# Wider weight loads for the scores, the transposes and the look-ahead rows, and a planner fed with measured durations

## The chip, the core and the metric

The kernel runs on one core of a Trainium2 chip. The metric is the device time of one execution in microseconds; lower is better. TensorE (PE) does the matmuls, VectorE (DVE), ScalarE (ACT) and GpSimd (POOL) the rest, SyncE (SP) issues the weight DMAs. A matmul on PE is a pair: a weight load, which puts the stationary operand (rows x columns) into the array, and the matmul, which streams the moving operand past it. The profile lists the two as PEld and PE.

## The reference

Four layers, applied one after the other on x of 2048 tokens x 640: A, B, A, B, each on a layer norm of x and added to x. B is a mixer MLP; A is attention in 64 segments of 32 tokens, where each segment also reads 8 memory rows that the segment before it produced. So the segments of one A layer can't run side by side.

```python
for s in range(n_seg):                       # 64 segments, in order
    h = concat([mem, x[segment s]])          # 8 + 32 = 40 rows x 640
    q, k, v = h @ Wq, h @ Wk, h @ Wv         # 32 heads of 192
    scores = where(mask, q @ k.T * 192**-0.5, -1e9)
    p = softmax(scores);  o = (p @ v) @ Wo
    mem = o[:8];  out.append(o[8:])
# B: h = gelu(ln(x) @ w1); four column groups of h shifted by -1, +1, -2, +2 tokens
#    x1 = x + shifted @ w2;  x + (x1 - x) + gelu(ln(x1) @ w3) @ w4
```

## The kernel before, in words

**Two lanes.** All four layers run in one pass. Lane 0 is the first A layer, lane 1 the second, five segments behind (`LAG`). Step t does segment t of lane 0 and segment t-5 of lane 1 together, so that each weight is loaded once for both. There are 69 steps: 0 to 4 have lane 0 alone, 5 to 63 have both, 64 to 68 have lane 1 alone. In a two-lane step a moving operand is N = NS = 80 columns wide (2 x 40), in a one-lane step N = 40. Every second step also runs one chunk of the B layers: 64 tokens of each lane, interleaved, so 128 rows.

**An attention step** (`attention_step`, L502) goes over four pairs of groups of four heads. For each group: 30 projection matmuls each for k, q and v (L532, weights 128x128, moving N columns); `pss`, the scores, six matmuls whose stationary operand is qT, N columns wide (L594); the masked minimum and scaling on DVE (L605), exp on ACT (L612), sums, reciprocal and product on DVE (L616 to L618); `pst`, four transposes of the probabilities, which load Pm as N x N weights (L626); the copy PT on ACT (L631); `pvt`, six transposes of v, which load vF N columns wide and stream 128 (L569); `pso`, eight matmuls with V as N x 128 weights (L640); the copy oT on DVE (L646); 30 output matmuls into `psy` (L657). qT, vF, Pm and PT exist once, kT, V twice, oT eight times. At the step's end ACT copies the new memory rows from `psy` to hT (L675), which the next step's first projection needs.

**The B chunk** (`chunk`, L812) transposes yTB (`psx`, L823) and, for the next chunk's first rows, the four columns behind it (`psl`, L830, weights 128 x 4 columns). The look-ahead rows lie in `lnx`: rows 0 to 3 the look-ahead, rows 32 to 95 the next segments of x; `psvl` (L880, through `transposes`, L722) transposes all 96 rows at once. Then w1, w2, w3, w4 (L905, L950, L985, L1011).

**What sets the order.** Nothing is issued as it stands in the source. Each operation is an entry `add(engine, duration, due, function, reads, writes)` of a `Plan` (L76). `place()` (L124) simulates all engines with these hand-written durations, with `LAT` between engines, `PE_LAT` behind PE, a DMA rate and the PSUM slots (six of class A, two of class B), and always takes the entry that can start first, by due time among those within 0.12 us on PE or 0.05 us elsewhere. The result is one fixed order for each engine. For a weight DMA that the plan starts at its own pace it adds a wait on the last PE operation that the plan has finished by then (L1105 to L1112), and a streamed DMA goes into a ring of eight slots. So a changed duration moves instructions on all five engines and the PE operations that release the weight DMAs. 31 streamed loads of 384 KB belong to each attention step; the other parts of the attention weights stay resident.

These lines carry the parts that the change touches:

```python
def mm_us(n, m=128, k=1):                     # L408, the plan's price of k matmuls
    return k * (max(54, n) / 2400.0 + 0.0025)
lhsT=q[:, c, 0:N], rhs=k_[:, j:j + w_, 0:N]   # L595, pss
transpose(out=o[0:N, i, 0:N], in_=Pb[0:N, i, 0:N], identity=ident[0:N, 0:N])   # L626, pst
lhsT=V_[0:N, ...], rhs=Pt[0:N, 2 * hf + i2, 0:N]                               # L640, pso
```

Of the kernel before, what the change touches and what calls it, by code (L numbers as in the profile page):

```python
# [30 lines left out]
LAT = 0.1  # L31
PE_LAT = 0.23
# [208 lines left out]
def kernel(  # L241
# [97 lines left out]
    nc.vector.memset(lnA[0:32, 0:1], 1.0 + EPS)  # L339
    nc.vector.memset(lnA[0:32, 1:2], EPS * EPS)  # L340

    hT = [ctile([P, KC, NS], bf16, f"hT{i}") for i in range(4)]
    qT = ctile([P, GC, NS], bf16, "qT")
    vF = ctile([P, GC, NS], bf16, "vF")
    kT = [ctile([P, 8, NS], bf16, f"kT{i}") for i in range(2)]
    Vt = [ctile([NS, 2 * VP], bf16, f"V{i}") for i in range(2)]
    Pm = ctile([NS, HG, NS], bf16, "Pm")
# [15 lines left out]
    lnx = h2u[0:96, Dm:2 * Dm]  # L363
# [9 lines left out]
    nc.gpsimd.memset(yTB[:], 0.0)  # L373
    nc.gpsimd.memset(xres[:], 0.0)
# [41 lines left out]


# [84 lines left out]
    def attention_step(t):  # L502
# [13 lines left out]
        def proj_pair(pr):  # L516
            s0 = base + sl * 2 * pr
            for kind, off in (("k", 0.0), ("q", 0.2), ("v", 0.5)):
                wbs, wv = load_pair(kind, pr, s0 + off * 2 * sl, LEAD_A)
                for j in range(2):  # L520
# [17 lines left out]
                    if kind == "q":  # L538
                        q = qT

                        def fq(op, pq=pq, q=q):
                            nc.scalar.copy(out=q[:, :, 0:N], in_=T(pq)[:, :, 0:N])  # L542
                        add("ACT", act_us(GC * N), due, fq, r=(pq,), w=(B("qT"),))
                    elif kind == "k":
                        k_ = kT[G % 2]

                        def fk(op, pq=pq, k_=k_):
                            p4 = T(pq)[:].rearrange("p (h c) n -> p h c n", h=2)
                            k4 = k_[:].rearrange("p (h c) n -> p h c n", h=2)
                            nc.vector.tensor_copy(out=k4[:, :, 0::3, 0:N], in_=p4[:, :, 0::2, 0:N])  # L550
                        add("DVE", dve_us(4 * N), due, fk, r=(pq,), w=(B("kT", G % 2, 0),))
                        for part, (r0, r1, jj) in enumerate(((0, 64, 1), (64, P, 2))):
                            def fk2(op, pq=pq, k_=k_, r0=r0, r1=r1, jj=jj):
                                p4 = T(pq)[:].rearrange("p (h c) n -> p h c n", h=2)
                                k4 = k_[:].rearrange("p (h c) n -> p h c n", h=2)
                                nc.vector.tensor_copy(out=k4[r0:r1, :, jj, 0:N], in_=p4[r0:r1, :, 1, 0:N])  # L556
                            add("DVE", dve_us(2 * N), due, fk2, r=(pq,), w=(B("kT", G % 2, 1 + part),))
                    else:
                        vf, V_ = vF, Vt[G % 2]

                        def fvf(op, pq=pq, vf=vf):
                            nc.scalar.copy(out=vf[:, :, 0:N], in_=T(pq)[:, :, 0:N])  # L562
                        add("ACT", act_us(GC * N), due, fvf, r=(pq,), w=(B("vF"),))
                        pvt = ps("A", [NS, GW], bf16, "pvt")

                        def fvt(op, pvt=pvt, vf=vf):
                            o = T(pvt)
                            for c in range(GC):
                                nc.tensor.transpose(out=o[0:N, c * P:(c + 1) * P], in_=vf[:, c, 0:N], identity=ident[:, :])  # L569
                        add("PE", mm_us(P, k=GC), due + 0.1 * sl, fvt, r=(B("vF"),), w=(pvt,))  # L570
                        for hf in range(2):
                            def fe(op, pvt=pvt, V_=V_, hf=hf):
                                src = T(pvt)[0:N, GWH * hf:GWH * (hf + 1)].rearrange("n (a b) -> n a b", a=2)
                                v0 = hf * (VP - 64)
                                dst = V_[0:N, v0:v0 + 512].rearrange("n (a b) -> n a b", a=2)[:, :, 64 * hf:64 * hf + Dh]
                                if hf:
                                    nc.vector.tensor_copy(out=dst, in_=src)
                                else:
                                    nc.scalar.copy(out=dst, in_=src)  # L579
                            add("DVE" if hf else "ACT", dve_us(GWH) if hf else act_us(GWH), due, fe, r=(pvt,),  # L580
                                w=(B("V", G % 2, hf),))

        def attend(g):
# [3 lines left out]
            pss = ps("A", [NS, HG * NS], f32, "pss")  # L587
            hi = s0 + 0.5 * sl

            def fs(op):  # L590
                o = T(pss)
                seq = [(0, 1, 0, 0), (1, 1, 2, 3), (2, 1, 3, 4), (3, 1, 5, 7), (0, 2, 1, 1), (2, 2, 4, 5)]
                for n_, (i, w_, c, j) in enumerate(seq):
                    nc.tensor.matmul(out=o[0:N, i * N:(i + w_) * N].rearrange("p (a b) -> p a b", a=w_),  # L594
                                     lhsT=q[:, c, 0:N], rhs=k_[:, j:j + w_, 0:N],  # L595
                                     start=(n_ == 0), stop=(n_ == len(seq) - 1), skip_group_check=True)
# [11 lines left out]
            add("DVE", dve_us(HG * N) + 0.1, hi - 4, f1, r=(pss,), w=(pss, smk))  # L608
# [4 lines left out]
            add("ACT", act_us(HG * N), hi - 4, f2, r=(pss, smk), w=(Pk,))  # L613
# [6 lines left out]
            add("DVE", 0.42 + 0.17 + 0.45, hi - 4, f3, w=(Pk, B("sm4", G % 2)))  # L620
            pst = ps("A", [NS, HG, NS], bf16, "pst")

            def f4(op):
                o = T(pst)
                for i in range(HG):
                    nc.tensor.transpose(out=o[0:N, i, 0:N], in_=Pb[0:N, i, 0:N], identity=ident[0:N, 0:N])  # L626
            add("PE", mm_us(N, N, 4), hi - 3, f4, r=(Pk,), w=(pst,))
            Pt = PT

            def f5(op):  # L630
                nc.scalar.copy(out=Pt[0:N, :, 0:N], in_=T(pst)[0:N, :, 0:N])  # L631
# [3 lines left out]
            def f6(op):  # L635
                o = T(pso)
                for hf in range(2):
                    for i2, col, c, st, sp in ((0, 0, 0, True, True), (0, 128, 1, True, False), (1, 192, 1, False, True),
                                               (1, 320, 2, True, True)):
                        nc.tensor.matmul(out=o[:, 3 * hf + c, 0:N], lhsT=V_[0:N, VP * hf + col:VP * hf + col + P],  # L640
                                         rhs=Pt[0:N, 2 * hf + i2, 0:N], start=st, stop=sp)
# [45 lines left out]
    def ln_ops(src, rows, st, stk, srck, due, const_cols):  # L687
# [16 lines left out]
        add("DVE", 2 * 0.47 + 0.19 + 0.28, due, f1, r=(srck,), w=(stk,))  # L704
# [5 lines left out]
        add("POOL", 0.7, due, f2, w=(stk,))  # L710

    def apply_ln(dst, src, rows, st, col, dstk, srck, stk, due, us=0.6):
# [12 lines left out]
    def gelu(pz, n, due, outs, w, a=(), own=None):  # L725
# [28 lines left out]
        add("DVE", dve_us(n * XB) + 0.15 * (len(outs) - 1), due, f4, r=(pz, gk), w=w)  # L754
# [8 lines left out]
    def chunk_loads(c, part):  # L763
# [23 lines left out]
        if edge:  # L787
            def fz(op):
                nc.gpsimd.memset(xres[:] if part == "x" else lnx[0:4, :], 0.0)
# [7 lines left out]
        for lane, k0 in look if part == "l" else ():  # L797
            def f(op, lane=lane, k0=k0):
                nc.gpsimd.dma_start(out=lnx[lane:4:2, :], in_=src[lane][k0:k0 + 2, :])
# [3 lines left out]
        if s < NSEG and part == "l":  # L803
            def f(op):
                nc.gpsimd.dma_start(out=lnx[32:96, :], in_=x0d[SEG * s:SEG * s + TOK, :])
# [6 lines left out]
    def chunk(c):  # L812
# [12 lines left out]
        psl = ps(PB, [4, KC, P], bf16, "psl")  # L825

        def ftl(op):
            o = T(psl)
            for m in range(KC):
                nc.tensor.transpose(out=o[:, m, :], in_=yTB[:, m, XB:XB + 4], identity=ident[:, :])  # L830
        add("PE", mm_us(128, k=KC), D(0.06), ftl, r=(B("yTB", 1),), w=(psl,))
# [3 lines left out]
        add("DVE", 0.81, D(0.05), fx, r=(ps1, B("xres")), w=(xk,))  # L835

        def fl(op):
            nc.vector.tensor_tensor(out=lnx[0:4, :], in0=T(psl)[:].rearrange("p k f -> p (k f)"), in1=lnx[0:4, :],
                                    op=ALU.add)
        add("DVE", 0.81, D(0.06), fl, r=(psl,), w=(B("lnx", "l"),))  # L840
# [3 lines left out]
        if not last:  # L844
            add("POOL", 0.3, D(0.1), fh, r=(B("yTB", 1),), w=(B("yTB", "h"),))
# [12 lines left out]
        def f1(op):  # L858
            srcv = lnx[0:96, :].rearrange("p (c f) -> p c f", c=2)
            for k in range(2):  # L860
                nc.vector.bn_stats(out=st2[0:96, 6 * k:6 * k + 6], in_=srcv[:, k, :])
            nc.vector.bn_aggr(out=st2[0:96, 12:14], in_=st2[0:96, 0:12].rearrange("p (c s) -> p c s", c=2))
            nc.vector.tensor_scalar(out=st2[0:96, 14:15], in0=st2[0:96, 13:14], scalar1=lnA[0:96, 0:1],
                                    scalar2=lnA[0:96, 1:2], op0=ALU.mult, op1=ALU.add)
        add("DVE", 2 * 0.47 + 0.19 + 0.14, D(0.07), f1, r=(B("lnx", "l"), B("lnx", "x")), w=(s2k,))

        def f2(op):
            nc.gpsimd.tensor_tensor(out=st2[0:96, 16:17], in0=st2[0:96, 14:15], in1=neghalf[0:96, 0:1], op=ALU.pow)
        add("POOL", 0.7, D(0.07), f2, w=(s2k,))
# [3 lines left out]
        def f3(op):  # L873
            nc.vector.tensor_scalar(out=vx[0:96, :], in0=lnx[0:96, :], scalar1=st2[0:96, 12:13],
                                    scalar2=st2[0:96, 16:17], op0=ALU.subtract, op1=ALU.mult)
# [3 lines left out]
        psl2 = ps(PB, [P, KC, 96], bf16, "psvl")  # L879
        transposes(psl2, vx, 96, D(0.11), (vxk,))  # L880
# [5 lines left out]
        def fel(op):  # L886
            nc.scalar.copy(out=vT[:, :, XB:XB + 4], in_=T(psl2)[:, :, 0:4])
        add("ACT", act_us(KC * 4), D(0.11), fel, r=(psl2,), w=(B("vTl"),))
        for j in range(2):
            s = 2 * c + 4 + j  # L890
            if s < NSEG:
                def fx0(op, s=s, j=j):
                    nc.scalar.copy(out=hT[s % 4][:, :, 0:SEG], in_=T(psl2)[:, :, 32 + SEG * j:32 + SEG * (j + 1)])
# [36 lines left out]
        if last:  # L930
# [4 lines left out]
            add("DVE", 0.6, D(0.4), fc2, w=(B("hTB", 0), B("hTB", 1)))  # L935
# [28 lines left out]
        add("DVE", 0.75, D(0.7), fxu, r=(uk,), w=(xk,))  # L964
# [118 lines left out]
    for t in range(T_A):  # L1083
# [4 lines left out]
        if t == T_A - 1:  # L1088
# [3 lines left out]
            add("POOL", 0.3, t * STEP, fh, r=(B("yTB", 1),), w=(B("yTB", "h"),))  # L1092
# [55 lines left out]
```

## Time and profile before

| | |
|---|---|
| median of 5 runs | 3554.52 us (3544.66 to 3561.55) |
| the profiled execution | 3556.94 us, its span 3555.2 us |
| PE busy, matmuls | 3389.2 us (95%), 84559 matmuls |
| PE weight loads busy | 3267.9 us, 84559 loads |
| DVE, ACT, POOL busy | 2479.8, 1519.9, 245.2 us |
| DMA | 1075.28 MB, mean 302 GB/s |
| mean granted PE clock | 0.976 |

Five of the 69 steps end (L683, the last copy of a step) at 99.6, 148.0, 198.1, 250.0 and 298.9 us: the one-lane steps of the start, the first of them behind the loading of the resident weights. The two-lane steps fill 298.9 to 3279.3 us, the one-lane steps of the end 3279.3 to 3524.0 us, and the last B chunk the rest. A two-lane step takes 50.5 us on average, a one-lane step behind the first 49 to 52 us, its last one 45.1.

How to read it: matmuls are pipelined, so the duration of one (about 200 ns) is not what it costs. What it costs is the distance from its start to the start of the next matmul, here called its pitch. The busy share of PE is a union of such durations and says little; the chain of waits, which gives each piece the time from its start to the next piece's, and the starts in the timeline give pitches.

### The profile page before, as it was taken

To read this page: it belongs to the slowest core of one execution; us is meant where nothing else is said; L and a number is where in the kernel's file an instruction comes from. 1 tells how busy PE (TensorE), PEld (TensorE's weight loads), DVE (VectorE), ACT (ScalarE), POOL (GpSimd) and SP (SyncE) were. 2 spreads that over 40 slices of the span, in tenths; PEclk is the share of its full clock that TensorE was granted. 3 is DMA by queue.
4 is the path that set the end of the run, shared out by engine and by line. 5 is a ranking of instruction groups with operands and counts; after the bars stand their busy time and mean duration, and the time that the engine had idled before them with its cause. 6 is when DMAs were issued, how large, how long until landed. Compare 5 with 4: busy or idle time off the path is not lost.

```text
span 3555.2 us, 188209 instructions
## 1 busy us (share of the span) xinstructions
PE 3389.2 (95%) x84559; PEld 3267.9 (92%) x84559; DVE 2479.8 (70%) x7433; ACT 1519.9 (43%) x3569; POOL 245.2 (7%) x488
## 2 busy tenths in 40 slices
PE   6989999999999999999999999999999999999886
PEld 5879999999999999999999999999999999999885
DVE  2556777777776777777777777777777777776554
ACT  1334444444444444444444444444444444444332
POOL 0000000000000000000000000000000000000000
PEclk7889999999999999999999999999999999999897
DMA  9988898889888988888888888898889888988895
GB/s 375 302 298 307 308 323 294 301 296 320 304 299 289 316 302 295 303 312 303 301 306 306 307 300 301 302 318 292 301 309 320 299 297 302 316 294 297 300 314 170
DMA packets 497753, 1075.28 MB, mean 302 GB/s; under 512 B 49454, under 2 KB 216892, under 8 KB 496944
## 3 DMA queue, kind: packets, MB, share of 16 engines
q1 hardware_dynamic: 489712, 1050.11, 85.5%
q8 instruction: 661, 10.83, 1.2%
q0 software_dynamic: 7232, 13.13, 1.2%
q14 instruction: 148, 1.21, 0.1%
HBM read 1057.79 MB, written 5.24 MB: 299 GB/s over the span
## 4 chain that ended last, share of the span: by engine, by line
PE 89%; DMA 4%; issue 2%; DVE 2%; ACT 1%; SPq 0%; POOL 0%; POOLq 0%; DVEq 0%; ACTq 0%
PE psq L532 16%; PE psk L532 16%; PE psv L532 15%; PE psy L657 15%; PE pvt L569 5%; PE pss L594 4%; PE pso L640 4%; PE psh L985 3%; PE y L1011 3%; PE pst L626 3%; DMA wst<-in_A_Wq_dram 2%; PE psh L905 1%; PE hs L950 1%; DMA wst<-in_A_Wk_dram 1%; PE psv L722 1%
## 5 line engine op out<-in xcount | busy, mean ns | idle before, releaser
L532 PEld LDWEIGHTS <-wst 128*128 128x128 bf16 x25668 | 1053.3, 100 | 44.0 <-issue 17.0
L657 PE MATMUL psy<-oT,wo 128*128 128x80 bf16 (+1 forms) x16560 | 685.1, 199 | 37.4 <-issue 22.0
L657 PEld LDWEIGHTS <-wo 128*128 128x128 bf16 x16560 | 622.0, 100 | 44.8 <-issue 32.1
L542 ACT CAST qT<-psq 128x480 bf16<-128x480 f32 (+1 forms) x552 | 292.4, 530 | 668.9 <-PE psq L532 665.2
L532 PE MATMUL psq<-hT,wst 128*128 128x80 bf16 (+1 forms) x9936 | 456.3, 199 | 10.7 <-DMA wst<-in_A_Wq_dram 7.2
L646 DVE CAST oT<-pso 128x480 bf16<-128x480 f32 (+1 forms) x552 | 340.9, 618 | 152.5 <-PE pso L640 142.3
L532 PE MATMUL psv<-hT,wv 128*128 128x80 bf16 (+1 forms) x9936 | 433.2, 199 | 11.3 <-issue 5.8
L532 PE MATMUL psk<-hT,wst 128*128 128x80 bf16 (+1 forms) x9108 | 438.9, 200 | 4.4 <-issue 2.8
L532 PEld LDWEIGHTS <-wv 128*128 128x128 bf16 x9936 | 385.1, 100 | 17.7 <-issue 6.7
L605 DVE CUSTOM_DVE_ANT_1 pss<-pss,mask 80x320 f32<-80x320 f32 (+1 forms) x512 | 242.8, 484 | 224.7 <-PE pss L594 128.7
L631 ACT COPY PT<-pst 80x320 bf16<-80x320 bf16 (+1 forms) x552 | 222.6, 403 | 404.1 <-PE pst L626 394.5
L532 PE MATMUL psv<-hT,wst 128*128 128x80 bf16 (+1 forms) x6624 | 368.2, 199 | 9.9 <-issue 8.1
L532 PE MATMUL psk<-hT,wk 128*128 128x80 bf16 (+1 forms) x7452 | 350.9, 199 | 15.6 <-ACT hT L675 10.8
L562 ACT CAST vF<-psv 128x480 bf16<-128x480 f32 (+1 forms) x552 | 290.7, 527 | 167.3 <-PE psv L532 165.7
L579 ACT COPY V<-pvt 80x384 bf16<-80x384 bf16 (+1 forms) x552 | 261.8, 474 | 222.4 <-PE pvt L569 213.6
L556 DVE CAST kT<-psk 64x160 bf16<-64x160 f32 (+1 forms) x1104 | 336.5, 305 | 8.3
L612 ACT ACTIVATE Pm<-pss,sm 80x320 bf16<-80x320 f32 (+1 forms) x552 | 279.2, 506 | 145.7 <-DVE sm L605 145.7
L532 PE MATMUL psq<-hT,wq 128*128 128x80 bf16 (+1 forms) x6624 | 319.8, 199 | 5.8 <-issue 3.1
L532 PEld LDWEIGHTS <-wk 128*128 128x128 bf16 x7452 | 299.6, 100 | 22.3 <-issue 21.9
L616 DVE TENSOR_REDUCE sm<-Pm 80x4 f32<-80x320 bf16 (+1 forms) x552 | 250.2, 453 | 87.0 <-ACT Pm L612 77.5
L550 DVE CAST kT<-psk 128x320 bf16<-128x320 f32 (+1 forms) x552 | 255.4, 463 | 72.6 <-PE psk L532 65.1
L569 PE MATMUL pvt<-ident,vF 128*80 128x128 bf16 (+1 forms) x3312 | 284.1, 223 | 5.6 <-ACT vF L562 2.5
(127 smaller groups left out, 4328.7 us busy)
## 6 DMA issues: line engine op xcount, KB each, us to landing
wst<-in_A_Wq_dram SPq DMA_DIRECT2D x828, 384.0 KB, 5.2
wst<-in_A_Wk_dram SPq DMA_DIRECT2D x759, 384.0 KB, 5.2
wst<-in_A_Wv_dram SPq DMA_DIRECT2D x552, 384.0 KB, 5.2
wstB<-in_B_w_dram SPq DMA_DIRECT2D x495, 320.0 KB, 5.0
wstB<-in_B_w_dram SPq DMA_DIRECT2D x132, 160.0 KB, 4.7
wo<-in_A_Wo_dram SPq DMA_DIRECT2D x8, 960.0 KB, 12.7
wv<-in_A_Wv_dram SPq DMA_DIRECT2D x4, 1152.0 KB, 11.7
wq<-in_A_Wq_dram SPq DMA_DIRECT2D x4, 768.0 KB, 11.7
```

Source lines behind the costliest of these rows:

```text
L532: nc.tensor.matmul(out=o[:, cc, 0:N], lhsT=wv(kc, GW * j + cc * P, GW * j + (cc + 1) * P), rhs=h[:, kc, c0:c0 + N], start=(kc == 0 and cc ...
L542: nc.scalar.copy(out=q[:, :, 0:N], in_=T(pq)[:, :, 0:N])
L550: nc.vector.tensor_copy(out=k4[:, :, 0::3, 0:N], in_=p4[:, :, 0::2, 0:N])
L556: nc.vector.tensor_copy(out=k4[r0:r1, :, jj, 0:N], in_=p4[r0:r1, :, 1, 0:N])
L562: nc.scalar.copy(out=vf[:, :, 0:N], in_=T(pq)[:, :, 0:N])
L569: nc.tensor.transpose(out=o[0:N, c * P:(c + 1) * P], in_=vf[:, c, 0:N], identity=ident[:, :])
L579: nc.scalar.copy(out=dst, in_=src)
L605: nc.vector.tensor_tensor_reduce(out=o, in0=o, in1=maskt.unsqueeze(1).to_broadcast([N, HG, N]), scale=-scale, scalar=3.0e38, op0=ALU.add, ...
L612: nc.scalar.activation(out=Pb[0:N, :, 0:N], in_=o, func=ACT.Exp, bias=sm_[0:N, 0:1], scale=-1.0)
L616: nc.vector.tensor_reduce(out=sm_[0:N, 2:2 + HG], in_=Pb[0:N, :, 0:N], axis=AX.X, op=ALU.add)
L646: nc.vector.tensor_copy(out=o_[:, :, 0:N], in_=T(pso)[:, :, 0:N])
L657: nc.tensor.matmul(out=o[:, m, c0:c0 + N], lhsT=wo[:, cc, m * P:(m + 1) * P], rhs=o_[:, cc, 0:N], start=st, stop=True, skip_group_check=True)
```

## The change

- `pss`: qT is now one flat tile; the weight load of chunk c takes 128 columns from the chunk's start (so 48 columns of the next chunk's, whose result rows nobody reads) for chunks 0 to 3, and 80 for chunks 4 and 5, in one-lane steps too.
- `pvt`: the same for vF: 128 columns for chunks 0 to 4, 80 for the last. `pst`: the same for Pm: 128 columns for three heads, 80 for the last; it always loads all 80 rows and streams 80 columns. `pso` always uses all 80 rows of V and PT. qT, vF and Pm are set to zero once at the start.
- `psl`: 68 columns (the 4 and the 64 before them) instead of 4, so its result lies in rows 64 to 67. `lnx` has 68 rows instead of 96: x in rows 0 to 63, look-ahead in 64 to 67; `psvl` transposes 68 rows.
- The planner's durations: LAT 0.1 to 0.12, PE_LAT 0.23 to 0.3, and the prices of 17 operations.

By the instruction order built from each kernel, 84559 matmuls stand in both. Of the 84559 weight loads, 9002 were narrower than 128 columns before (1450 of them 40 columns or fewer), and 2378 are after, none under 68.

```diff
-LAT = 0.1
-PE_LAT = 0.23
+LAT = 0.12
+PE_LAT = 0.3
...
-    qT = ctile([P, GC, NS], bf16, "qT")
-    vF = ctile([P, GC, NS], bf16, "vF")
+    qTw = ctile([P, GC * NS], bf16, "qT")
+    qT = qTw[:].rearrange("p (c n) -> p c n", c=GC)
+    vFw = ctile([P, GC * NS], bf16, "vF")
+    vF = vFw[:].rearrange("p (c n) -> p c n", c=GC)
...
-    lnx = h2u[0:96, Dm:2 * Dm]
+    lnx = h2u[0:TOK + 4, Dm:2 * Dm]
...
+    def wide(c, n):
+        return P if c < n - 1 else NS
...
-                        pvt = ps("A", [NS, GW], bf16, "pvt")
+                        pvt = ps("A", [P, GW], bf16, "pvt")
...
-                                nc.tensor.transpose(out=o[0:N, c * P:(c + 1) * P], in_=vf[:, c, 0:N], identity=ident[:, :])
+                                w_ = wide(c, GC)
+                                nc.tensor.transpose(out=o[0:w_, c * P:(c + 1) * P], in_=vFw[:, c * NS:c * NS + w_],
+                                                    identity=ident[:, :])
...
-                            add("DVE" if hf else "ACT", dve_us(GWH) if hf else act_us(GWH), due, fe, r=(pvt,),
+                            add("DVE" if hf else "ACT", 0.35 if hf else act_us(GWH), due, fe, r=(pvt,),
...
-                    nc.tensor.matmul(out=o[0:N, i * N:(i + w_) * N].rearrange("p (a b) -> p a b", a=w_),
-                                     lhsT=q[:, c, 0:N], rhs=k_[:, j:j + w_, 0:N],
+                    m_ = wide(c, GC - 1)
+                    nc.tensor.matmul(out=o[0:m_, i * N:(i + w_) * N].rearrange("p (a b) -> p a b", a=w_),
+                                     lhsT=qTw[:, c * NS:c * NS + m_], rhs=k_[:, j:j + w_, 0:N],
...
-            add("DVE", dve_us(HG * N) + 0.1, hi - 4, f1, r=(pss,), w=(pss, smk))
+            add("DVE", dve_us(HG * N) + 0.02, hi - 4, f1, r=(pss,), w=(pss, smk))
...
-            add("ACT", act_us(HG * N), hi - 4, f2, r=(pss, smk), w=(Pk,))
+            add("ACT", act_us(HG * N) + 0.09, hi - 4, f2, r=(pss, smk), w=(Pk,))
...
-            add("DVE", 0.42 + 0.17 + 0.45, hi - 4, f3, w=(Pk, B("sm4", G % 2)))
-            pst = ps("A", [NS, HG, NS], bf16, "pst")
+            add("DVE", 0.53 + 0.0085 * N, hi - 4, f3, w=(Pk, B("sm4", G % 2)))
+            pst = ps("A", [P, HG, NS], bf16, "pst")
...
-                    nc.tensor.transpose(out=o[0:N, i, 0:N], in_=Pb[0:N, i, 0:N], identity=ident[0:N, 0:N])
-            add("PE", mm_us(N, N, 4), hi - 3, f4, r=(Pk,), w=(pst,))
+                    w_ = wide(i, HG)
+                    nc.tensor.transpose(out=o[0:w_, i, :], in_=Pmw[:, i * NS:i * NS + w_], identity=ident[0:NS, 0:NS])
+            add("PE", mm_us(NS, N, 4), hi - 3, f4, r=(Pk,), w=(pst,))
...
-                        nc.tensor.matmul(out=o[:, 3 * hf + c, 0:N], lhsT=V_[0:N, VP * hf + col:VP * hf + col + P],
-                                         rhs=Pt[0:N, 2 * hf + i2, 0:N], start=st, stop=sp)
+                        nc.tensor.matmul(out=o[:, 3 * hf + c, 0:N], lhsT=V_[:, VP * hf + col:VP * hf + col + P],
+                                         rhs=Pt[:, 2 * hf + i2, 0:N], start=st, stop=sp)
...
-        add("DVE", 2 * 0.47 + 0.19 + 0.28, due, f1, r=(srck,), w=(stk,))
+        add("DVE", 1.37, due, f1, r=(srck,), w=(stk,))
...
-        add("DVE", dve_us(n * XB) + 0.15 * (len(outs) - 1), due, f4, r=(pz, gk), w=w)
+        add("DVE", dve_us(n * XB) + 0.235 * (len(outs) - 1), due, f4, r=(pz, gk), w=w)
...
-                nc.tensor.transpose(out=o[:, m, :], in_=yTB[:, m, XB:XB + 4], identity=ident[:, :])
-        add("PE", mm_us(128, k=KC), D(0.06), ftl, r=(B("yTB", 1),), w=(psl,))
+                nc.tensor.transpose(out=o[0:TOK + 4, m, :], in_=yTB[:, m, XB - TOK:XB + 4], identity=ident[:, :])
+        add("PE", mm_us(128, k=KC), D(0.06), ftl, r=(B("yTB", 0), B("yTB", 1)), w=(psl,))
...
-        add("DVE", 0.81, D(0.05), fx, r=(ps1, B("xres")), w=(xk,))
+        add("DVE", 0.49, D(0.05), fx, r=(ps1, B("xres")), w=(xk,))
...
-        transposes(psl2, vx, 96, D(0.11), (vxk,))
+        transposes(psl2, vx, TOK + 4, D(0.11), (vxk,))
```

## The prediction

> **What bounds the kernel now.** I read the page's busy shares first, then its slices, then single stages, then the chain of waits and the starts on PE in short windows.
>
> ```profile
> PE   6989999999999999999999999999999999999886
> PEclk7889999999999999999999999999999999999897
> DMA  9988898889888988888888888898889888988895
> ```
>
> PE is busy everywhere, but the DMA engines stand near nine tenths too. So a faster PE gains only until the weight stream is the limit. Stage by stage (one-lane, two-lane, one-lane; columns: length, PE, PEld, DVE, ACT, POOL busy, clock, DMA share, GB/s):
>
> ```profile
> 148.00:198.10 50.10, 45.04 (x1221) 41.11 (x1219) 28.79 (x108) 19.79 (x58) 1.14 (x3) 0.90 0.90 301
> 1461.00:1511.00 50.00, 49.78 (x1254) 49.12 (x1251) 38.48 (x113) 25.11 (x58) 1.14 (x3) 1.00 0.89 305
> 3279.30:3328.90 49.60, 45.91 (x1257) 41.84 (x1255) 29.35 (x110) 19.94 (x57) 1.13 (x3) 0.94 0.91 303
> ```
>
> A two-lane step is PE's: hardly any gap, full clock. A one-lane step has half the columns to stream, yet takes as long, with PE idle for 4 to 5 us and the clock partly throttled. Pitches tell why. In the two-lane stretch 300 to 3260 us the median pitch of a projection matmul (80 columns) is 36 ns, of a 128-column one 56, of a 320-column one 136: columns at 2.4 per ns plus 2.5. In one-lane steps 40 columns take 25 ns. Summing these over the order of matmuls gives 47.6 and 48.7 us for two-lane steps in turn (measured: 50.5 on average), but only 36 us for one-lane steps (measured: about 50). The starts in a one-lane step at full clock (start, busy, then the group):
>
> ```profile
> 207.14 0.70 PE L1011 MATMUL y<-wstB,h2u 128*128 128x320 bf16 x4
> 207.77 0.27 PE L626 MATMUL pst<-ident,Pm 40*40 40x40 bf16 x4
> 207.97 0.47 PE L532 MATMUL psk<-hT,wst 128*128 128x40 bf16 x12
> 208.41 0.50 PE L569 MATMUL pvt<-ident,vF 128*40 128x128 bf16 x6
> 208.84 0.47 PE L532 MATMUL psk<-hT,wst 128*128 128x40 bf16 x12
> ```
>
> Four `y` matmuls take 4 x 136 = 0.54 us, so pst could start at 207.68; it starts at 207.77. Four pst of 25 ns end at 207.87; the next group starts at 207.97. The same at pvt: 6 x 56 = 0.34, but 0.43 us to the next start. Every change between 128-column weights and weights of 64 columns or rows at most costs 84 to 96 ns, in and out. In two-lane steps only psl does so:
>
> ```profile
> 1552.63 0.81 PE L532 MATMUL psq<-hT,wst 128*128 128x80 bf16 x18
> 1553.37 0.44 PE L830 MATMUL psl<-ident,yTB 128*4 128x128 bf16 x5
> 1553.75 0.60 PE L532 MATMUL psq<-hT,wq 128*128 128x80 bf16 x12
> ```
>
> 18 x 36 = 0.65 us, so 0.09 us lost going in; 5 x 56 = 0.28 of the 0.38 us behind it, so 0.10 lost coming out.
>
> **Part 1: the changes of shape go away.** The program of before states each matmul's tile of the array: 580 changes along PE's order, one in the program after, since apart from five matmuls at the start no load has under 68 columns or rows. Of the 580, 45 lie before 99.6 us, behind the loading of the resident weights: worth nothing. 58 lie in the two-lane stretch (29 psl): excess read from the starts 5.6 us, on a PE that is never slack: -5.6. 477 lie in the nine other one-lane steps; at the median of 87 to 93 ns they cost 44.5 us (longer excesses, which are waits for data, cut off at 110 ns). Back come 288 pst transposes in these nine steps that stream 80 instead of 40 columns, 11 ns each: +3. So PE's work there shrinks by 41 us, 4.6 per step.
>
> How much of it reaches the end is the open point. Against: the streams move 301 to 303 GB/s, 15.1 MB a step; the best 50 us stretch with streaming (280 to 330 us) shows 330 GB/s at a 0.96 share, so 15.1 MB need 45.7 us: a floor for these steps of 50, i.e. at most 4.3 x 9 = 39 us. Also, PE idles there already[...]. For: SP's queue waits mostly for PE in these steps too (some 120 of 190 us between 110 and 300 us), so DMAs start when PE has come far enough, and a PE that comes sooner starts them sooner. The ends are 0 and -39; I take the middle, -20, 2.2 us a step, since neither resource is alone the limit.
>
> The Trainium skill speaks against the widening twice. TensorEngine Tiling (Array Packing), Overview: for dimensions of 64 or less the array splits into tiles, for up to twice the throughput. Here the small groups are alone between 128x128 ones, and nothing runs beside them; the rows above show the loss instead, which the page's Key Properties names too (changing the mode drains the array). By the speedup one would keep the narrow forms; by the rows they cost 44.5 us.
>
> **Part 2: 80-column loads become 128 columns.** From the duration of single loads (out<-in, shape, count | busy, mean ns):
>
> ```profile
> L657 PEld LDWEIGHTS <-wo 128*128 128x128 bf16 x16560 | 622.0, 100 | 44.8 <-issue 32.1 <-DMA wo<-in_A_Wo_dram 10.1
> L569 PEld LDWEIGHTS <-vF 128*80 128x80 bf16 x2832 | 180.3, 118 | 1.9 <-issue 1.8
> L594 PEld LDWEIGHTS <-qT 128*80 128x80 bf16 x2832 | 148.3, 121 | 6.5 <-issue 2.3 <-ACT qT L542 0.7
> L626 PEld LDWEIGHTS <-Pm 80*80 80x80 bf16 x1888 | 111.1, 119 | 20.0 <-DVE Pm L618 10.9 <-issue 0.5
> ```
>
> TensorE: Matmul & The Clock Gate, LDWEIGHTS (loading the stationary operand), says a load takes columns / 1.2 ns: 67 for 80 columns, 107 for 128. Were that the pitch, 12 widened loads in each of 472 two-lane groups would turn pitches of 36 to 69 ns into 107: about 12 x 472 x 60 = +340 us. But loads of 128 columns follow each other at 36 ns in the projections, and last 100 ns, less than the 118 to 121 of 80 columns; that page's section on Fast Weight Load says that 128 bf16 columns are read by a faster path. The rows decide: a wide load costs nothing beyond its matmul. What 80 columns cost is small, since loads overlap matmuls: the excess over the ideal pitch, averaged over 470 groups, is 27 ns for a pss group, 14 for pst, 8 for pvt, together 23 us, the most this part can give. Two of six pss loads, the last pst and the last pvt load stay at 80, and pso, with 128-column loads already, also shows 4 ns at its first matmul, so that much of it is waiting for a semaphore. By position I take 16 + 7 + 2 = 25 ns x 472 = -12 us (bounds 0 and -23).
>
> psvl streams 68 instead of 96 columns: 5 x 12 ns x 29 = -1.7. Zeroing three tiles at the start (DVE) lies under the loading of the first 90 us; if it didn't, under 2 us. DVE and ACT do the same work on as many columns. psl now reads both halves of yTB, but psx, ahead of it on PE, already waited for both; POOL's queue gets the same loads in number and size.
>
> **Part 3: the new plan.** No work changes, only orders. PE waits in the two-lane stretch, from the starts: pst for Pm 18.3 us, the step boundary for hT (L675) 13.9, weights about 14, pso for PT 7.6, and some 35 us in waits that name nobody. In the two orders I summed pitches between producer and consumer. Boundary: 0 and 557 ns in turn, the same in both; stays. pst to pso: 108 of 432 groups had 643 ns and waited 83, so about 726 are needed; after, 27 groups lie below, at 536: 27 x 190 = 5.1 against 7.7, so -2.6. From the PE operation that releases a streamed DMA to its first use: shortest 5.4 us before, 5.9 after (28 loads under 5.5 become none); median landing 5.2 us: -4 of the 14. pss to pst: shortest 2974 before, 3316 after; -5, because the 18 us are DVE's and ACT's order, which PE distances don't settle. Any of these can turn, and a changed order can open a new wait: as bounds I take the whole 40 us of named waits that are not the boundary as gain, and as much as loss. My value: -8 (the -12 above less 4 for what opens).
>
> **Sum.** -20 - 5.6 - 12 - 1.7 - 8 = -47 on the profiled execution of 3556.9 us (span 3555.2 and 1.7 around it): 3510. The median of the runs is 2.4 lower, 0.07%; I keep 3510.
>
> **Rivals.** *A: the weight stream holds the one-lane steps.* They keep 50 us, the stall moves from PE's shape changes to waits for wst. For: DMA share 0.90, 301 GB/s. Against: 330 GB/s were seen. Then -27: 3530. *B: PE alone holds them, and the plan helps.* -39 in one-lane steps, -20 by the plan: 3479. For: SP waits for PE. *C, slower: the new order makes pst late.* Place: pst (L626) waits for DVE's product (L618), behind the single Pm, and everything on PE queues behind it, and with PE the release of weight DMAs. Before, one of 16 groups of a two-step period waits 255 ns on average (often 365). Price at 365 ns: 365 x 29.5 periods = 10.8 us per group of the 16. From five late groups the 47 us are eaten; eight give 3510 + 86 = 3596. Against: all distances there grew. That the widening doesn't work as said (128 columns loading slowly) I exclude by the projections' 36 ns.
>
> **Chances.** Forecast 3510: 0.58; A 0.20; B 0.12; C 0.10. Range: from 3472 (B with the full load gain of part 2) to 3548 (A with nothing from part 2 or the plan, less its psl), which leaves out most of C and the far end of B. A measurement can tell 0.3% (11 us) from no change: 3544 to 3565. Faster gets the forecast, B and most of A: 0.84; same 0.07; slower 0.09.
>
> **What would show it.** Right: no psl, pst or pvt start delayed by 0.09 us; a pss group's pitches at 36 and 69 ns; one-lane steps of 47 to 48 us; two-lane steps of 50.0. A shows as one-lane steps of 50 with PE waiting for wst at a DMA share still at 0.9; C as more than 18 us of pst waiting for DVE Pm. Wrong altogether would be 128-column loads of qT, vF or Pm lasting over 121 ns, or two-lane steps above 50.5 us.

## The result, and the profile after

The changed kernel takes 3541.35 us (median of 30 runs, 3528.73 to 3559.56), the kernel before 3555.66 (51 runs, 3542.56 to 3567.51). The ratio is 0.9961, with a 95% interval of 0.9951 to 0.9970: faster by 0.4%, 14 us where 47 were forecast. The profiled execution took 3545.44 us, its span 3543.7, its mean granted clock 0.979 (before 0.976). The time lies inside the range, near its slow end, but that end was set for another cause (rival A).

The page of after, slices first and then the shares of the chain that ended last:

```profile
PE   5889999999999999999999999999999999999886
PEclk8899999999999999999999999999999999999997
DMA  9999898889888988888889888988899888988995
...
PE 89%; DMA 4%; issue 4%; DVE 1%; ACT 1%; SPq 0%; POOL 0%; POOLq 0%; DVEq 0%; ACTq 0%
```

"issue" is time in which PE waited for nothing that the profile shows. It is 4% of the chain; before it was 2%, and DVE, now 1%, was 2%. The DMA engines are as full as before. The step ends listed ahead of the prediction (99.6 to 3524.0 us) lie 10.6 us later than the same copies on the profile's own axis (89.0 to 3513.4). The stretches of both kernels are set by such ends; each is one step long, so it holds one step's work, begun a fifth of a step late. The three stages (columns as in the prediction: length, PE, PEld, DVE, ACT, POOL busy, clock, DMA share, GB/s):

```profile
146.50:195.50 49.00, 40.41 (x1195) 39.17 (x1195) 27.84 (x104) 18.55 (x54) 1.21 (x3) 0.90 0.92 308
1455.90:1505.40 49.50, 49.48 (x1262) 48.99 (x1259) 38.05 (x113) 24.63 (x56) 1.14 (x3) 1.00 0.91 312
3272.20:3321.50 49.30, 40.88 (x1232) 39.29 (x1229) 28.55 (x107) 19.28 (x56) 1.13 (x3) 0.94 0.92 300
```

In a one-lane step PE is busy for 4 to 5 us less than before (40.4 and 40.9 against 45.0 and 45.9), and still the stage is not shorter by that: the idle time took most of it. The clock in these two stages is 0.90 and 0.94 as before, though PE now idles 8.4 to 8.6 us there, where it was 3.7 to 5.1. From one step's last copy out of `psy` to the next step's, one-lane steps take 48.6 us (before 49.8), two-lane steps 50.48 (before 50.51). Split at such copies, the four one-lane steps from 89 us on shrank by 4.9 us, the 59 two-lane steps by 2.0 and the five one-lane steps behind them by 6.5; the tail grew by 2.0.

The starts on PE in a one-lane step of after (start, busy, then the group):

```profile
203.65 1.25 PE L1024 MATMUL y<-wstB,h2u 128*128 128x320 bf16 x8
204.74 0.31 PE L639 MATMUL pst<-ident,Pm 80*128 80x80 bf16 x4
204.88 0.50 PE L579 MATMUL pvt<-ident,vF 128*128 128x128 bf16 x6
205.22 0.31 PE L541 MATMUL psv<-hT,wst 128*128 128x40 bf16 x6
```

Eight `y` matmuls at 136 ns are 1.09 us, and pst starts 1.09 us after them; four pst at 36 ns are 0.14, six pvt at 56 ns 0.34, and the next groups start 0.14 and 0.34 us on. The 0.09 us at each change of shape are gone. Single loads (count | busy, mean ns):

```profile
L579 PEld LDWEIGHTS <-vF 128*128 128x128 bf16 x2760 | 173.4, 100 | 16.6 <-issue 10.7 <-ACT vF L571 2.9 <-DVE kT L565 0.5
L606 PEld LDWEIGHTS <-qT 128*128 128x128 bf16 x2208 | 140.1, 101 | 10.3 <-issue 7.1 <-ACT qT L551 3.0
L639 PEld LDWEIGHTS <-Pm 80*128 80x128 bf16 x1656 | 100.0, 100 | 12.3 <-DVE Pm L630 4.9 <-issue 4.7
```

The widened loads last 100 ns where those of 80 columns lasted 118 to 121. So the work on PE did what was forecast. What ate it is in the waits. PE's waits by what ended them (us in total, times, longest), before:

```profile
PE psy L657 <- issue: 22.0, 31, 2.3
PE psv L532 <- issue: 14.0, 16, 1.8
PE psk L532 <- issue: 7.1, 8, 1.8
PE psq L532 <- issue: 6.4, 8, 1.5
```

and after:

```profile
PE psv L541 <- issue: 25.6, 30, 2.2
PE psy L670 <- issue: 23.8, 40, 2.0
PE psk L541 <- issue: 17.3, 21, 2.3
PE psq L541 <- issue: 11.5, 21, 1.2
PE pvt L579 <- issue: 9.1, 6, 2.7
PE pso L653 <- issue: 7.6, 7, 1.9
PE pss L606 <- issue: 6.6, 7, 2.1
```

All such rows together went from 63 to 115 us. They can fall in the middle of a group of matmuls. One of them, on PE, a little ahead of the starts above:

```profile
201.21 0.81 PE L670 MATMUL psy<-oT,wo 128*128 128x40 bf16 x26
203.39 0.27 PE L670 MATMUL psy<-oT,wo 128*128 128x40 bf16 x4 [1.37 <-issue]
```

The 27th of 30 matmuls that all read the resident tile `wo` and one `oT` stands 1.37 us, though its data were there when the 26 ahead of it ran. The DMA queues between 200.8 and 201.0 us show what was late:

```profile
q8 instruction: 1, 0.02, 28.7%
```

One packet of queue 8, 16 KB, begins there and lasts 0.92 us. PE goes on 1.6 us after it has landed. Over the whole run this queue carries

```profile
q8 instruction: 661, 10.83, 1.2%
```

661 packets, 10.83 MB. PE runs 84559 matmuls, as many loads and some 150 instructions for semaphores (136 in before, 171 in after): over these, 10.83 MB are 64 bytes for each. So the queue carries PE's instructions, and a packet of 16 KB is a block of 256 of them, 128 matmuls with their loads: some 5 us of work.

I took from both traces the matmuls that start over 100 ns late and wait for no semaphore: 74 us in 125 stalls before, 136 us in 188 after. Of these, 84% before and 96% after (96 and 99% of the time) end 1.15 to 1.70 us after such a packet has landed (median 1.42); of moments taken at random 10% lie in that interval. The place of a stall in PE's program says the same without any time: number all of PE's instructions in order, loads, matmuls and semaphore waits, and count them modulo 256. All 89 stalls over 200 ns in before and all 154 in after then fall on number 192 or 193, and so do those of every kernel below. So they stand at the border between two blocks, and these are waits for late instruction blocks.

In the two-lane steps the books balance. The lateness of all starts against the ideal pitches, summed, is 133 us in before and 134 in after, but its make-up is not the same: waits for semaphores (over 100 ns) fell from 55 to 37 and the small losses below 100 ns from 37 to 12, which is 43 us of gain; block waits grew from 41 to 84, which is 43 us of loss.

### The profile page after: what moved, and what is told of

Same layout as the page of the kernel before. It is cut to its first block, busy times and chain, and to the rows that moved or that the text cites. A ratio compares the mean times of both kernels' runs of the same rounds, so it can differ in the third digit from the quotient of the medians.

```text
span 3543.7 us, 188048 instructions
## 1 busy us (share of the span) xinstructions
PE 3326.2 (94%) x84559; PEld 3234.3 (91%) x84559; DVE 2470.6 (70%) x7436; ACT 1520.4 (43%) x3569; POOL 247.2 (7%) x488
## 3 DMA queue, kind: packets, MB, share of 16 engines
q8 instruction: 661, 10.83, 1.2%
## 4 chain that ended last, share of the span: by engine, by line
PE 89%; DMA 4%; issue 4%; DVE 1%; ACT 1%; SPq 0%; POOL 0%; POOLq 0%; DVEq 0%; ACTq 0%
PE psy L670 16%; PE psk L541 16%; PE psq L541 16%; PE psv L541 15%; PE pvt L579 5%; PE pso L653 4%; PE pss L606 4%; PE psh L998 3%; PE y L1024 3%; PE pst L639 2%; DMA wst<-in_A_Wk_dram 1%; PE psh L918 1%; PE hs L963 1%; DMA wst<-in_A_Wv_dram 1%; PE psv L735 1%
## 5 line engine op out<-in xcount | busy, mean ns | idle before, releaser
L541 PEld LDWEIGHTS <-wst 128*128 128x128 bf16 x25668 | 1031.9, 100 | 40.2 <-issue 27.7
L541 PE MATMUL psq<-hT,wst 128*128 128x80 bf16 (+1 forms) x9936 | 466.4, 199 | 11.5 <-issue 7.5
L541 PE MATMUL psk<-hT,wst 128*128 128x80 bf16 (+1 forms) x9108 | 429.2, 199 | 11.5 <-issue 8.2
L541 PE MATMUL psv<-hT,wst 128*128 128x80 bf16 (+1 forms) x6624 | 323.4, 199 | 9.5 <-issue 9.0
L588 DVE COPY V<-pvt 80x384 bf16<-80x384 bf16 (+1 forms) x552 | 188.6, 350 | 192.1 <-PE pvt L579 109.6
L579 PE MATMUL pvt<-ident,vF 128*128 128x128 bf16 x3312 | 283.4, 223 | 12.9 <-issue 9.1
```

The lines of the kernel that those rows point to most:

```text
L541: nc.tensor.matmul(out=o[:, cc, 0:N], lhsT=wv(kc, GW * j + cc * P, GW * j + (cc + 1) * P), rhs=h[:, kc, c0:c0 + N], start=(kc == 0 and cc ...
L579: nc.tensor.transpose(out=o[0:w_, c * P:(c + 1) * P], in_=vFw[:, c * NS:c * NS + w_], identity=ident[:, :])
```

## The experiments

**Theory F**: what the change takes off PE returns as late instruction blocks. PE comes sooner to the next block, and the blocks have to come beside 300 GB/s of weights. **Rival R**: the new plan gives back what the wide loads gain. **Rival A**, from the prediction: the weight stream alone holds the one-lane steps. The first four kernels ran on one chip, the last four on another, each four beside runs of the kernel before.

### 1 and 2: each half of the change alone

wide_only is the change with the planner's old durations; plan_only is the kernel before with the new ones. Three of the durations, as plan_only changes them (wide_only has them the other way round in after):

```
-            add("DVE", dve_us(HG * N) + 0.1, hi - 4, f1, r=(pss,), w=(pss, smk))
+            add("DVE", dve_us(HG * N) + 0.02, hi - 4, f1, r=(pss,), w=(pss, smk))
...
-            add("ACT", act_us(HG * N), hi - 4, f2, r=(pss, smk), w=(Pk,))
+            add("ACT", act_us(HG * N) + 0.09, hi - 4, f2, r=(pss, smk), w=(Pk,))
...
-            add("DVE", 0.42 + 0.17 + 0.45, hi - 4, f3, w=(Pk, B("sm4", G % 2)))
+            add("DVE", 0.53 + 0.0085 * N, hi - 4, f3, w=(Pk, B("sm4", G % 2)))
```

> The wide loads and the 68-column psl with the planner's old durations; ACT, SP and POOL keep the order of before, PE all but a few places. Theory F (PE's own instructions arrive too late: a 16 KB block for every 128 matmuls, and every wait that goes away elsewhere lets PE run into the next block sooner): the waits for instructions grow by 20 to 40 us, the pst waits for DVE stay near 18 us, and the time falls by 10 to 25 us only (ratio 0.993 to 0.997). Rival R (the new plan's order and releases made the block waits grow; the loads themselves gave all they should): the full 40 us or more of the loads show, ratio 0.985 to 0.989, and block waits stay near those of before.

> Before with the new planner durations alone, all loads narrow as before. Theory F: the 18 us of pst waits for DVE go, block waits grow by about as much, ratio 0.998 to 1.003. Rival R: block waits grow by 30 us or more and the kernel is slower, ratio 1.005 to 1.010.

wide_only took 3535.91 us, 0.9960 of before (0.9942 to 0.9978); plan_only 3539.40, 0.9972 (0.9956 to 0.9987). Before took 3548.8 on that chip. R falls: the plan alone gains 9 us, and the loads without the plan gain 13, not 39. Neither gives anything back to the other by its order; yet the two together gain 14. In both the stalls grow as F wants: 74 us before, 100 in wide_only, 103 in plan_only, 136 with both. For plan_only neither expectation was met in full: its stalls grew by 29 us where F had about 18 and R 30 or more, and it is a little faster than F's 0.998, where R had it slower.

### 3 and 4: the same two kernels with a lighter stream

Each streamed DMA of an attention weight brings half its columns, 192 instead of 384 KB, and the second group of a pair uses the first group's columns. So half of these weights are left out and other values are computed; instructions, their order and all else stay.

```
-                nc.sync.dma_start(out=T(b)[:, 0:PW], in_=w_src[kind][:, kc, cols])
+                nc.sync.dma_start(out=T(b)[:, 0:PW // 2], in_=w_src[kind][:, kc, PW * pr:PW * pr + PW // 2])
...
-            return T(slots[kc - nres])[:, c0:c1]
+            return T(slots[kc - nres])[:, c0 % GW:c0 % GW + c1 - c0]
```

> Before, but every streamed attention weight DMA brings half of its columns (192 KB instead of 384), and the second group of a pair uses the first one's columns; all orders and all matmuls are as before. So the weight traffic falls by about 40% while PE's work stays. Theory F with a full DMA system as the reason for late blocks: block waits fall from 80 us to under 30, time falls by 50 to 90 us. If blocks were late by themselves, whatever else moves: block waits stay, and only the waits for weights (some 15 to 25 us) go.

> After, with the same halved streams. Theory F with a full DMA system: block waits fall from 150 us to under 40, and the distance to half_before opens from the 14 us of the full streams to 45 us or more. If the one-lane steps alone are held by the weight stream (rival A of the prediction): the distance opens in the one-lane steps only, by about 25 us, and the two-lane steps keep 50.5 us. If blocks were late whatever else moves: distance stays near 14 us.

half_before took 3442.97 us, 0.9697 (0.9682 to 0.9712), 106 us less than before where F had 50 to 90; half_after 3375.98, 0.9508 (0.9493 to 0.9522). The distance between the two kernels is now 67 us, where it was 14. The stalls without a semaphore fell to 3 us in half_before and 11 in half_after. The page of half_after, slices and totals:

```profile
DMA  9676666666666666666666666666666666666774
...
DMA packets 497752, 654.72 MB, mean 194 GB/s; under 512 B 49454, under 2 KB 490684, under 8 KB 496944
```

The DMA engines stand at six to seven tenths with as many packets. The clock in the two-lane steps is 1.00 in all four kernels, so it does not make their difference. PE's longest waits in half_before (us in total, times, longest):

```profile
PE psk L532 <- ACT hT L675: 10.8, 35, 0.3
PE pst L626 <- DVE Pm L618: 9.2, 41, 0.4
```

and in half_after:

```profile
PE psk L541 <- ACT hT L688: 10.8, 35, 0.3
PE psy L670 <- DMA wo<-in_A_Wo_dram: 7.4, 5, 1.5
PE pso L653 <- ACT V L590: 5.9, 8, 0.9
PE psv L735 <- DVE vbg L887: 5.6, 5, 4.5
PE psv L541 <- DMA wv<-in_A_Wv_dram: 5.1, 4, 2.8
PE psx L735 <- DVE vbg L727: 4.7, 1, 4.7
PE hs L963 <- issue: 4.6, 1, 4.6
PE pst L639 <- DVE Pm L630: 4.1, 9, 1.0
```

Of the waits for nothing one is left near the top: a single one of 4.6 us at hs, which before has too (4.4 us). The rest has names: the step boundary (hT) as before, and pst for DVE at less than half. The packets of instruction blocks are no faster (0.98 to 0.99 us at the median); they start sooner. In two-lane steps a block's packet starts, at the median, 78 matmuls ahead of the one at its border, where the stalls stand, in before, 74 in after, and 112 in both half_before and half_after: some 34 to 38 matmuls, or 1.3 us of work, more in hand. Told from the other end: from the moment when PE begins the block ahead of it, it takes 2.1 us in before and 2.4 in after until a block's packet starts, and 0.7 us in the two lighter kernels. Hardly any packet starts more than 128 matmuls ahead (none in after, 22 of 661 in half_after, the earliest at 139): the look-ahead that these traces show is about one block, some 5 us.

A falls as the only cause: of the 67 us, two-lane steps give most (49.54 to 48.74 us each, 47.6 in all), one-lane steps 22. What the lighter stream changes besides (PE's waits for DMAs fall by 18 us from before to half_before, by 13 from after to half_after) is far less than the distance it opens. The runs also lie closer together: a standard deviation of 1.5 us in both (4 runs each), where before and after have 6.6 and 7.1.

### 5 and 6: the terms of the sum, with the lighter stream

half_wide is wide_only with the lighter stream. half_one is half_before with 80 columns or rows in one-lane steps for pss, pvt, pst and pso only (the three tiles zeroed once), neither wider loads nor a new plan:

```
-                    nc.tensor.transpose(out=o[0:N, i, 0:N], in_=Pb[0:N, i, 0:N], identity=ident[0:N, 0:N])
+                    nc.tensor.transpose(out=o[:, i, :], in_=Pb[:, i, :], identity=ident[0:NS, 0:NS])
```

> The wide loads and wide psl with the old planner durations, on halved weight streams (the second group of a pair uses the first one's streamed columns). The terms of the prediction's sum without the plan, with no late blocks in the way: one-lane steps about -18 us (what half_after showed there), two-lane loads -12, psl and psvl -7, so about 3406 us beside 3443 of half_before; the pst waits for DVE stay at 20 us. Under the rival reading (it is the plan that brings the 67 us) it stays above 3425.

> half_before with one part of the change: the stationary operands of pss, pvt, pst and pso are 80 columns and rows in one-lane steps too; no load of 128 for them, psl and plan as before. If the changes of the array's shape are what the one-lane steps lose: about 18 us, 3425, with two-lane steps unchanged at 49.5. If the one-lane gain came from elsewhere: 3440 or more.

half_wide took 3403.26 us, 0.9577 (0.9555 to 0.9598); half_one 3422.45, 0.9633 (0.9611 to 0.9654). Against half_before (on the other chip) that is -40 and -20.5. In half_one the one-lane stages give 6.8 and 13.0 us, the two-lane ones 1.1. In half_wide the two-lane ones give 20.4. Both came out as expected (3406 and 3425). Behind half_wide's 40 the plan brings 27 more to half_after.

### 7 and 8: the same bytes, released at another time

The weights' DMAs in after are let go when PE has come to a certain operation. Both kernels keep every instruction and its place on PE, DVE, ACT, POOL and SP, and shift only that operation. In the traces' two-lane steps a weight DMA is then issued, at the median, 16 matmuls (0.6 us of PE's work) earlier than in after, or 18 (0.7 us) later.

```
-            while k >= 0 and done[k].end + PE_LAT > o.start:
+            while k >= 0 and done[k].end + PE_LAT > o.start - 1.5:
```

pace_late has `o.start + 1.0` there.

> After, in the same order on every engine, but each paced weight DMA waits for a PE operation that the plan has ending 1.5 us sooner: it is released some 0.9 us of PE work earlier, so more bytes are in flight, with the same bytes in all. If the depth of what is queued makes instruction blocks late: block waits rise by 20 us or more and the kernel gets slower (ratio to before 0.998 to 1.004). If only bytes per time matter: same as after within 5 us.

> After, same order, each paced weight DMA released some 0.8 us of PE work later. If depth makes blocks late: block waits fall by 20 us or more, waits for weights rise by less, the kernel is faster than after (ratio to before 0.988 to 0.994). If only bytes per time matter: waits for weights come on top, ratio 0.996 to 1.002.

pace_early took 3599.58 us, 1.0130 (1.0106 to 1.0154): slower than before, with all of the change in it, and by more than the 1.004 at most that was expected. pace_late took 3528.37 (3516.17 to 3532.82), 0.9932 (0.9912 to 0.9952): faster than before, and than after too, though its interval touches that of after (0.9951 to 0.9970). PE's waits in pace_early:

```profile
PE psy L670 <- issue: 34.2, 44, 2.2
PE psv L541 <- issue: 33.0, 35, 2.8
PE psq L541 <- issue: 26.1, 34, 2.2
PE psk L541 <- issue: 21.2, 20, 2.5
PE pso L653 <- issue: 13.5, 16, 2.0
```

and in pace_late:

```profile
PE psv L541 <- issue: 19.5, 21, 2.2
PE psy L670 <- issue: 17.6, 25, 2.6
PE psq L541 <- issue: 13.6, 18, 2.0
PE psk L541 <- issue: 13.2, 12, 2.2
PE psk L541 <- ACT hT L688: 10.8, 35, 0.3
PE pvt L579 <- issue: 7.3, 7, 1.9
PE psq L541 <- DMA wst<-in_A_Wq_dram: 6.2, 17, 0.7
```

Block stalls are 177, 136 and 99 us in pace_early, after and pace_late. The spans are 3585.7, 3543.7 and 3514.4: +42 and -29 us for +41 and -37 us of stalls, less 11 us of new waits for weights (29 to 40 us) in the later one. Both profiled executions are the fastest of their runs, and that of after is slower than its median; by the medians the distances from after are +58 and -13, and by the ratios to before, which was run on each chip, +60 and -10. Neither more bytes nor another order is needed to move the stalls; when the weights are released is enough.

A table of what the runs say together (block stalls over 100 ns in us; us per two-lane step; in one-lane steps at the start of the kernel and at its end, without the first and the last step):

| kernel | median us | block stalls | two-lane | one-lane |
|---|---|---|---|---|
| before | 3555.66 | 74 | 50.51 | 49.8, 49.9 |
| after | 3541.35 | 136 | 50.48 | 48.6, 48.6 |
| wide_only | 3535.91 | 100 | 50.26 | 48.5, 48.1 |
| plan_only | 3539.40 | 103 | 50.43 | 49.3, 48.8 |
| half_before | 3442.97 | 3 | 49.54 | 44.3, 45.8 |
| half_one | 3422.45 | 7 | 49.52 | 42.6, 42.8 |
| half_wide | 3403.26 | 12 | 49.20 | 42.5, 43.2 |
| half_after | 3375.98 | 11 | 48.74 | 42.8, 42.8 |
| pace_early | 3599.58 | 177 | 51.08 | 49.4, 49.5 |
| pace_late | 3528.37 | 99 | 49.96 | 48.5, 49.4 |

## Why the prediction was half right

**Part 1, the changes of shape: right in the mechanism, and right in size only where the stream is light.** The losses of 0.09 us are gone from the starts (measured for weights of 4 and 40 columns among those of 128). The value of -20 for the one-lane steps was a middle between 0 and -39, struck for the full stream, and there the changed kernel shows -11.4. That half_one shows -20 with the lighter stream is luck; why not even that stream gives the whole 41 us stays open. The -5.6 for psl was right: the late starts of psl and of the matmul behind it sum to 5.6 us in two-lane steps of before and to nothing in after.

**Part 2, the wider loads: right.** The rule of the Trainium skill that a load takes columns / 1.2 ns (TensorE: Matmul & The Clock Gate, LDWEIGHTS (loading the stationary operand)), which the prediction set aside, does not fit the rows of after: 100 ns at 128 columns, less than the 118 to 121 at 80. Parts 1 and 2 were priced at 39.3 us together; half_wide against half_before shows 40, of them 20.4 in two-lane steps, where 12 + 5.6 + 1.7 = 19.3 were forecast.

**Part 3, the plan: right in sign, too small.** It was priced at -8; with the lighter stream it brings 27. The term that was mis-sized is pss to pst, left at -5 of 18 because PE's distances do not settle DVE's order. From the starts, pst's late entries in the two-lane stretch cost 23 us in half_before and 1.2 in half_after. The -2.6 for pso was about right (8.6 to 5.5), and so was the boundary, which stayed (14.3 in both).

**The step that failed** is in part 3: "and some 35 us in waits that name nobody". They were put into the list of what PE waits for and then left out of the sum, as if they stayed at 35 whatever PE does. They were waits for instruction blocks, and grew from 41 to 84 us in the two-lane stretch, from 74 to 136 over the whole run. The parts as the lighter stream measures them are -67, and -75 without the 8 us of stalls that half_after has more than half_before; with +62 that leaves -13, where -14 was measured by the medians and -11.5 by the spans. Most of the miss lies in the two-lane steps (-2.0 where -27.3 was forecast), the rest mainly in the one-lane ones (-11.4 for -20). The Trainium skill has the structure in Runtime: NRT & Kernel Launch, Instruction fetch mechanics: instructions come in 16 KiB blocks of 256 while the engine executes, over a DMA queue of its own. It adds that crossing a block's border is mostly hidden. At 190 to 194 GB/s the trace agrees (3 to 12 us in some 3400), at 303 GB/s it does not: up to 2.8 us in a single stall of after, 136 in all.

**The ends of the range** do not come out of the prediction's own terms: B with the full load gain is 3468, not 3472, and A with nothing from part 2 or the plan lies near 3550, not at 3548. The measured time is inside either way.

**The rivals.** A was half right: in one-lane steps the idle time moved and the DMA share is 0.92. But PE's wait was not for wst, and most of the loss lies in two-lane steps, of which A says nothing. B's 39 us appear nowhere. C is refuted: pst's waits for DVE fell, from 18.3 us in two-lane steps to 1.2. None of the three had the cause. Of the signs set down, the starts came as said; the steps did not: 48.6 us instead of 47 to 48, 50.48 instead of 50.0.

**What stays open.** The trace does not show when PE asks for a block, only when its packet starts. The tail's 2.0 us more are not explained. The lighter stream changes the depth of queued weights and the share of the DMA engines at once; the paced kernels show that timing alone moves the stalls, not through which queue or engine a block is held up. That a block waits behind queued weights is argued from that, not shown. Wide loads with the old durations and a later release together were not tried.

## What to carry to other kernels

Waits on the busiest engine that name nobody are not a constant of the kernel: look whether they end a fixed time after a packet of the engine's own instructions, and whether they stand at one place modulo the block's 256 instructions, and give them a line in the sum, since work taken off that engine can come back there. Where weights stream at the limit, try a later release: here 0.7 us later gained 13 us by the medians, and 0.6 us earlier cost 58, more than the change gained. To see what an edit is worth without this, run both kernels with fewer bytes and the same instructions.

## What was not expected of the hardware

A block's packet lasts 0.98 to 1.01 us at the median whether the stream moves 194 or 303 GB/s; only its start moves, from 0.7 us (half_after) to 2.4 us (after) behind the moment when PE begins the block ahead of it. PE goes on some 1.4 us after it has landed, so a block that starts late costs up to 2.9 us at a stretch (pace_early). And the lighter stream takes away most of the spread between runs: a standard deviation of 6.6 us in before, 1.5 in half_before.
